# A fused decode attention kernel: the first load of B's output weights as transfers of 64, 51 and 13 rows

## The chip, the cores and the metric

The kernel runs on one core of one Trainium2 chip. The metric is the device time of one execution in microseconds (us), taken as the median of several runs. A second source is the profile: one execution recorded by the hardware profiler, with a start time and a duration for the instructions of every engine and for the packets of the DMA queues. In the profile PE is TensorE (PEld its weight loads), DVE is VectorE, ACT is ScalarE, POOL is GpSimd and SP is SyncE, which in this kernel does little but issue DMA transfers. A "q" behind an engine's name is its sequencer, so SPq is SP issuing a transfer or waiting on a semaphore. The core has 16 DMA engines; the page gives their mean busy share.

## What is computed

Two attention layers of one decode step, one after the other, their outputs set side by side. Both have a batch of 4, one query position, a model width of 512, 32 query heads of width 128 and a cache of 8192 positions. Layer A has 8 key/value heads, each shared by 4 query heads, and looks only at the last 2048 positions (`W`). Layer B has 32 key/value heads and looks at all 8192.

```python
def _B_ref(x, k_cache, v_cache, wq, wo):
    q = (x @ wq).reshape(B, Sq, H, Dh) ...            # 4 x 1 x 512 times 512 x 4096
    scores = jnp.einsum("bhqd,bhkd->bhqk", q, k_cache) * (Dh ** -0.5)
    p = _softmax(scores, axis=-1)
    o = jnp.einsum("bhqk,bhkd->bhqd", p, v_cache)
    return o ... .reshape(B, Sq, H * Dh) @ wo         # 4096 x 512 output weights
# _A_ref is the same with k and v cut to the last W positions and repeated over 4 query heads
return jnp.concatenate([a, b], axis=-1)
```

All tensors are bf16. B's keys and values alone are 537 MB, read once.

## The kernel before

**Chunks.** The work is cut into 40 chunks. Chunks 0 to 7 (`c < NCA`) are A's eight key/value heads, all four batch rows at once. Chunks 8 to 39 are B's: four heads (`hq` counts the groups of four heads) of one batch row, so that four chunks in a row share one `hq`. A chunk's keys are loaded to `kv` in SBUF, transposed on PE against an identity matrix (`emit_T`, line 555, matmuls of line 501), copied from PSUM to `kt` by DVE or ACT (lines 578 and 576), and multiplied with the query (`emit_S`, line 595, matmuls of line 503). Then come the softmax statistics, the exponentials, and the product with the values (`emit_pv`, line 747).

**Output weights.** B's `wo` is used in pieces of 512 rows, one for each `hq`. `dma_wos` (line 367) loads such a piece to the tile `wos`: 128 partitions, four weight rows of 512 in each, so one partition's row is 4096 bytes and one load is 512 KB. `reorder` (line 834) of each B chunk multiplies `wos` with a selection matrix `back` on PE, and `take_wol` copies the result to `wol`; `emit_fin` multiplies the chunk's attention output with `wol` at the chunk's end. A's own output weights go to the tile `wor` by `dma_wo` (line 359), also 512 KB a load.

**Order of loads.** SP issues nearly every transfer, in an order that is written out in lines 468 to 489: A's keys, values and output weights first, then for each B chunk the keys (`dma_kB`) and the values (`dma_vB`), with `dma_wos` ahead of the keys of every fourth B chunk. At the very end stand the output weights of A's last two heads (`LATEWO`). A transfer that reuses a buffer waits on SP for the engine that frees it, and everything behind it on SP waits too. `dma_wos(0)`, which has nothing to wait for, stands behind the values of A's chunk 7 and ahead of the keys of chunk 8, which are loaded as three pieces.

**Completion.** Each transfer raises a semaphore by 16 when it has landed. `add_dma` (line 93) counts the uses of a semaphore, and a key names the count at which a load is complete. POOL waits for these counts and passes them on to PE through counters (`land_wos`, `land_kB`, `land_vB`, issued by `relay` at line 82), one load after the other in the order of chunks. PE waits for `("wr", c)`, the counter that `land_wos` raises, ahead of the first reorder matmul of a chunk.

Of the kernel before, what the change touches and what calls it, by code (L numbers as in the profile page):

```python
# [13 lines left out]
P = 128  # L14
# [3 lines left out]
NH = 10  # L18
NWO = 2
LATEWO = 2  # L20
NPB = 2
NSM = 2
SLAG = 2
# [155 lines left out]
def bass_concat_heads__sliding_block_cached__mha_block_cached__decode_kernel(  # L179
# [30 lines left out]
    NCA = Hkv  # L210
# [13 lines left out]
    sch = _Sched()  # L224
    with ExitStack() as es:
        block = es.enter_context(nc.Block())

        def sb(name, shape, dt):
            return es.enter_context(nc.sbuf_tensor(name, shape, dt))

        def ps(name, shape, dt):
# [4 lines left out]
        wos = sb("wos", [P, 4, DO], BF16)  # L236
# [29 lines left out]
        pm = sb("pm", [P, HB, NB, 4], F32)  # L266
        pbt = {0: sb("pba", [P, NPB, NTA * 16 + NW], BF16), 1: sb("pbb", [P, 2, NTB * 2 + NW], BF16)}
        oT = sb("oT", [P, NSM, 16], BF16)
# [35 lines left out]
            waits=["c_onesf", "c_identf"], key="c_ind")  # L304
# [45 lines left out]
        def dma_wq(ab, at):  # L350

            waits = take(("wq", ab), at, 2, ("qmm", ab))
            src = WQ[ab].rearrange("(p r) n -> p (r n)", r=KC)
            sch.add_dma("sp", lambda e: e.dma_start(flat(at, 2), src), "d_h%d" % at, waits=waits, key=("wq", ab))
# [4 lines left out]
        def dma_wo(g):  # L359

            src = A_wo[g * 4 * P:(g + 1) * 4 * P, :].rearrange("(p r) n -> p (r n)", r=4)
            slot = wo_slot(g)
            dst = wor[:, slot, :]
            sch.add_dma("sp", lambda e: e.dma_start(dst, src), "d_wo%d" % slot,
                        waits=[("fin", g - 2)] if g >= 2 else [], key=("wo", g))

        def dma_wos(hq):


            src = B_wo[4 * hq * P:4 * (hq + 1) * P, :].rearrange("(p r) n -> p (r n)", r=4)  # L370
            sch.add_dma("sp", lambda e: e.dma_start(wos[:, :, :].rearrange("p r n -> p (r n)"), src), "d_wos",
                        waits=[("reord", NCA + 4 * hq - 1, 3)] if hq else [], key=("wos", hq))

        def dma_A(kind, c):
            ch = chunks[c]
# [62 lines left out]
        def dma_vB(c):  # L438

            ch = chunks[c]  # L440
            src = B_v[ch["b"], 4 * ch["hq"]:4 * ch["hq"] + 4].rearrange("u (pp j) d -> (u pp) (j d)", pp=P // 4)
            dst = flat(VB, 4)
            pieces = vpieces(c)
            fam = "d_v%d_" % len(pieces)
            j0 = 0
            for i, n in enumerate(pieces):
                waits = held[4] + held[5] + held[6] + held[7] if c == NCA else [("pv", c - 1, 0 if j0 + n <= NTB // 2 else 1)]
                x = slice(j0 * P, (j0 + n) * P)
                sch.add_dma("sp", lambda e, x=x: e.dma_start(dst[:, x], src[:, x]), fam + str(i), waits=waits, key=("v", c, i))
                j0 += n  # L450
# [21 lines left out]
        for c in range(NCA):  # L472
# [3 lines left out]
            if c == 2:  # L476
                dma_wq(1, 6)
            if c != 1 and c < NCA - LATEWO:
                dma_wo(c)
# [3 lines left out]
        for c in range(NCA, NC):  # L483
            if (c - NCA) % NB == 0:
                dma_wos((c - NCA) // NB)
            dma_kB(c)
            dma_vB(c)
        for c in range(NCA - LATEWO, NCA):
            dma_wo(c)
# [9 lines left out]
        def pe_mm(o, l, r, start=True, stop=True, transpose=False, waits=(), key=None):  # L499
            if transpose:  # L500
                sch.add("pe", lambda e: e.transpose(o, l, r), waits, key)  # L501
            else:
                sch.add("pe", lambda e: e.matmul(o, l, r, start=start, stop=stop), waits, key)  # L503
# [223 lines left out]
        def spread_A(c, bs):  # L727

            for b in bs:
                sch.add("act", lambda e, b=b: e.activation(  # L730
                    probs_of(c).rearrange("p j (b c) -> p j b c", b=NB)[:, :, b, :], eA[:, c % 2, :].rearrange("p (j c) -> p j c", c=REP),
                    ACTF.Copy, scale=mk[:, b:b + 1]),
                    waits=[("exp1", c), "mk", ("c_pb", 0)] + ([("pv", c - NPB)] if c >= NPB else []) if b == 0 else [],
                    key=("exp", c) if b == NB - 1 else None)
# [117 lines left out]
        def emit_fin(c):  # L852
            ab = 0 if c < NCA else 1
            if ab == 1:
                ov = oz[:, :].rearrange("p (b u) -> p b u", b=NB)
                ops = [(ov[:, :, u], wol[:, u, :]) for u in range(4)]
                waits = ["c_oz", ("oT", c)]
            else:
                w = wor[:, wo_slot(c), :].rearrange("p (r n) -> p r n", r=4)
                ops = [(zA[:, c % 2, r * NB:(r + 1) * NB], w[:, r, :]) for r in range(4)]  # L860
                waits = [("z", c), ("wo", c)]

            for i, (l, r) in enumerate(ops):
                for h, (p0, x) in enumerate(out_halves(ab)):
                    pe_mm(fin[p0:p0 + NB, 0:DO // 2], l, r[:, x], start=False,
                          stop=i == len(ops) - 1 and c == NCA - 1, waits=waits if i == h == 0 else [],
                          key=("fin", c) if i == len(ops) - 1 and h == 1 else None)
# [172 lines left out]
        for p0, x in out_halves(1):  # L1040
            pe_mm(fin[p0:p0 + NB, 0:DO // 2], zz[:, :], sel4[:, 0:2, :].rearrange("p r x -> p (r x)"), start=False, key=("end", p0))
        for c in range(NCA - LATEWO, NCA - 1):
            emit_fin(c)
# [62 lines left out]
```

## Time and profile before

| what | value |
|---|---|
| median of 3 runs | 1369.17 us |
| lowest and highest run | 1368.85 and 1373.74 us |
| time of the profiled execution | 1368.99 us |
| span of the profiled execution (first to last instruction) | 1367.3 us |
| mean granted TensorE clock | 0.976 |
| PE busy, ACT busy, DVE busy (share of the span) | 89%, 41%, 54% |
| bytes read from HBM | 587.21 MB |

The profiled execution's own time is 1.69 us over its span, for what lies around the instructions, and 0.18 us under the median. The kernel moves 587 MB through the DMA engines, so the first things to read are the DMA engines' busy share and rate over the span, and then where PE waits for a load to land. Shares of a short window can come out above 1.00, since a packet is counted in the window in which it starts.

### The profile page before, as it was taken

The page shows a single profiled execution, that of the slowest core. Times are in us where ns is not written, and L with a number is a line of the kernel's source. Part 1 is how long each engine was busy: PE and PEld are TensorE (multiplying, and loading weights), DVE is VectorE, ACT ScalarE, POOL GpSimd, SP SyncE. Part 2 cuts the span into 40 slices and gives each one's busy share as a digit, 9 for nine tenths or more (in the row PEclk, how much of TensorE's full clock was granted, in tenths as well). Part 3 has the DMA queues.
Part 4 walks back from the last instruction along what each step waited for, and adds up shares of the span by engine and source line. Part 5 has one row for each costly group of instructions (what it writes and reads, how often), then busy time and mean ns, then how long its engine had stood idle before and what let it go on. Part 6 is the DMA issues. An engine that isn't in the chain of part 4 may idle for free.

```text
span 1367.3 us, 62934 instructions
## 1 busy us (share of the span) xinstructions
PE 1222.9 (89%) x27807; PEld 1126.6 (82%) x27843; DVE 731.9 (54%) x1495; ACT 555.0 (41%) x777; POOL 202.8 (15%) x84
## 2 busy tenths in 40 slices
PE   6688799989898999888989899889899898899998
PEld 5687698878887988888889888878898888888888
DVE  2575455545455555554555555545555555455565
ACT  2453344434344443333444344334444343344443
POOL 2000022222210222222101222221012222200000
PEclk9998999999999999999999999999999999999999
DMA  9999999999999999999999999999999999999998
GB/s 398 428 427 431 432 438 431 428 435 424 441 431 429 431 429 437 435 432 429 437 430 437 429 429 431 439 433 429 429 439 435 429 430 437 439 428 429 429 427 372
DMA packets 16629, 587.52 MB, mean 430 GB/s; under 512 B 1864, under 2 KB 1888, under 8 KB 3936
## 3 DMA queue, kind: packets, MB, share of 16 engines
q1 hardware_dynamic: 16576, 587.21, 99.7%
q8 instruction: 15, 0.25, 0.1%
q14 instruction: 6, 0.05, 0.0%
q10 hardware_dynamic: 32, 0.01, 0.0%
HBM read 587.21 MB, written 0.01 MB: 429 GB/s over the span
## 4 chain that ended last, share of the span: by engine, by line
DMA 57%; PE 38%; issue 2%; DVE 2%; ACT 1%; SPq 0%; ACTq 0%; POOLq 0%; DVEq 0%
DMA kv<-in_B_k_cache_dram 51%; PE tr L501 22%; PE sc L503 10%; DMA kv<-in_A_k_cache_dram 4%; PE tr L503 3%; DMA kv<-in_B_v_cache_dram 2%; PE po L503 2%; PE ms L503 1%; PE fin L503 0%; DVE kt L578 0%; DVE sA L631 0%; ACT pbb L700 0%; PE sc L933 0%; ACT pba L730 0%; PE ms L501 0%
## 5 line engine op out<-in xcount | busy, mean ns | idle before, releaser
L501 PE MATMUL tr<-identb,kv 128*128 128x128 bf16 x8704 | 672.1, 223 | 48.5 <-POOLq L82 35.7
L578 DVE COPY kt<-tr 128x1024 bf16<-128x1024 bf16 x736 | 502.8, 691 | 320.3 <-PE tr L501 317.1
L501 PEld LDWEIGHTS tr<-identb,kv 128*128 128x128 bf16 x8704 | 520.9, 100 | 60.3 <-issue 52.0
L576 ACT ACTIVATE kt<-tr 128x1024 bf16<-128x1024 bf16 x352 | 359.3, 1023 | 455.4 <-PE tr L501 453.2
L503 PE MATMUL sc<-qq,kt 128*128 128x64 bf16 x8192 | 401.1, 192 | 11.1 <-DVE kt L578 9.4
L503 PEld LDWEIGHTS sc<-qq,kt 128*128 128x128 bf16 x8192 | 330.7, 98 | 17.7 <-DVE kt L578 12.7
L425 POOL COPY kv<-kv 128x4096 int32<-128x4096 int32 x54 | 193.0, 3602 | 988.4 <-DMA kv<-in_B_k_cache_dram 988.4
L700 ACT ACTIVATE pbb<-sc,negb 32x128 bf16<-32x128 f32 x256 | 137.9, 539 | 134.3 <-DVE negb L682 131.5
L503 PE MATMUL tr<-pbb,kv 128*128 128x64 bf16 x4096 | 135.8, 193 | 28.1 <-ACT pbb L700 25.5
L503 PEld LDWEIGHTS tr<-pbb,kv 128*128 128x128 bf16 x4096 | 131.1, 99 | 31.9 <-issue 29.7
L503 PE MATMUL po<-pbb,kv 128*128 128x64 bf16 x4096 | 135.0, 194 | 4.3 <-issue 4.3
L503 PEld LDWEIGHTS po<-pbb,kv 128*128 128x128 bf16 x4096 | 127.5, 98 | 5.4 <-issue 4.4
L848 ACT ACTIVATE wol<-tr 128x512 bf16<-128x512 f32 x32 | 19.1, 597 | 203.4 <-PE po L503 203.4
L850 DVE CAST wol<-tr 128x512 bf16<-128x512 f32 x64 | 41.2, 686 | 54.8 <-PE tr L503 54.8
L933 PE MATMUL sc<-sel,identb 128*128 128x512 bf16 x167 | 51.1, 384 | 13.6 <-issue 13.6
L933 PEld LDWEIGHTS sc<-sel,identb 128*128 128x128 bf16 x167 | 16.2, 97 | 48.6 <-issue 38.5
L707 DVE TENSOR_REDUCE rs<-pbb 128x4 f32<-128x512 bf16 x32 | 22.0, 687 | 50.1 <-ACT pbb L700 50.1
L780 DVE RECIPROCAL ib<-ms 128x8 f32<-128x8 f32 x32 | 6.6, 208 | 58.1 <-PE ms L503 58.1
L503 PE MATMUL tr<-wos,back 32*128 32x512 bf16 x384 | 34.8, 383 | 0.6 <-issue 0.5
L503 PE MATMUL po<-wos,back 32*128 32x512 bf16 x128 | 33.9, 384 | 0.0
L668 DVE TENSOR_REDUCE gm<-ms 4x4 f32<-4x128 f32 x72 | 19.8, 275 | 23.3 <-PE ms L501 23.3
L648 DVE TENSOR_REDUCE rh<-sc 128x4 f32<-128x512 f32 x32 | 22.1, 692 | 14.3 <-PE sc L503 14.3
(92 smaller groups left out, 506.2 us busy)
## 6 DMA issues: line engine op xcount, KB each, us to landing
kv<-in_B_v_cache_dram SPq DMA_DIRECT2D x10, 4096.0 KB, 24.1
kv<-in_B_k_cache_dram SPq DMA_DIRECT2D x7, 4096.0 KB, 19.7
kv<-in_A_k_cache_dram SPq DMA_DIRECT2D x8, 2048.0 KB, 15.8
kv<-in_A_v_cache_dram SPq DMA_DIRECT2D x8, 2048.0 KB, 16.7
kv<-in_B_k_cache_dram SPq DMA_DIRECT2D x6, 2048.0 KB, 26.2
kv<-in_B_v_cache_dram SPq DMA_DIRECT2D x3, 2048.0 KB, 29.9
kv<-in_A_wq_dram SPq DMA_DIRECT2D x1, 4096.0 KB, 12.5
wor<-in_A_wo_dram SPq DMA_DIRECT2D x8, 512.0 KB, 21.2
```

The costliest lines, as they stand in the source:

```text
L425: sch.add("pool", lambda e, dst=dst, org=org: e.tensor_copy(dst, org), waits=[("T", s0 + ch["NG"] - 1)] if g == QC[0] else [])
L501: sch.add("pe", lambda e: e.transpose(o, l, r), waits, key)
L503: sch.add("pe", lambda e: e.matmul(o, l, r, start=start, stop=stop), waits, key)
L576: sch.add("act", lambda e: e.activation(dst, src, ACTF.Copy), waits=waits, key=("ev", s))
L578: sch.add("dve", lambda e: e.tensor_copy(dst, src), waits=waits, key=("ev", s))
L648: sch.add("dve", lambda e: e.tensor_reduce(out=dst, in_=src, axis=AX.X, op=ALU.max), waits=[("S", ch["s"] + (half + 1) * ch["NG"] // 2 - 1 ...
L668: sch.add("dve", lambda e: e.tensor_reduce(out=gm[0:C, m, 0:U], in_=src, axis=AX.X, op=ALU.max), waits=[key_of("trm", c, half)], key=key_o ...
L700: sch.add("act", lambda e, src=src, dst=dst, pp=pp, u=u: e.activation(dst, src, ACTF.Exp, bias=negb[pp, half, u:u + 1], scale=scale), wait ...
L707: sch.add("dve", lambda e: e.tensor_reduce(out=dst, in_=probs_of(c, half).rearrange("p j u -> p u j"), axis=AX.X, op=ALU.add), waits=[("ex ...
L848: sch.add("act", lambda e, u=u, o=o: e.activation(wol[:, u, :], o, ACTF.Copy), waits=[("reord", c, u)], key=("wol", c, u))
L850: sch.add("dve", lambda e, u=u, o=o: e.tensor_copy(wol[:, u, :], o), waits=[("reord", c, u)], key=("wol", c, u))
L933: return e.matmul(sc[:, 1, :], identb[:, :], sel4[:, :, :].rearrange("p r x -> p (r x)"), start=True, stop=True)
```

## The change

The first load of `wos` (`hq` of 0) is issued as three transfers in place of one: partitions 0 to 63, 64 to 114 and 115 to 127. All three raise the semaphore `d_wos`, and the key that `land_wos` waits for stands on the third, so the count waited for is 48 where it was 16. The seven later loads of `wos` stay one transfer each; the counts that they are waited for at are 32 higher. The bytes, their places in SBUF, the queue (SP) and the place in the order of loads stay the same.

```diff
+UNEVEN = (64, 51, 13)
...
             src = B_wo[4 * hq * P:4 * (hq + 1) * P, :].rearrange("(p r) n -> p (r n)", r=4)
-            sch.add_dma("sp", lambda e: e.dma_start(wos[:, :, :].rearrange("p r n -> p (r n)"), src), "d_wos",
-                        waits=[("reord", NCA + 4 * hq - 1, 3)] if hq else [], key=("wos", hq))
+            dst = wos[:, :, :].rearrange("p r n -> p (r n)")
+            waits = [("reord", NCA + 4 * hq - 1, 3)] if hq else []
+            if hq == 0:
+                rows = 0
+                for n in UNEVEN:
+                    x = slice(rows, rows + n)
+                    rows += n
+                    sch.add_dma("sp", lambda e, x=x: e.dma_start(dst[x, :], src[x, :]), "d_wos", key=("wos", hq) if rows == P else None)
+                return
+            sch.add_dma("sp", lambda e: e.dma_start(dst, src), "d_wos", waits=waits, key=("wos", hq))
```

## The prediction

> **What bounds the kernel now.** I read the page's span and DMA lines first, then the busy shares by stretch, then the chain of waits, and last SP's timeline around the changed load.
>
> ```profile
> span 1367.3 us, 62934 instructions
> ...
> DMA packets 16629, 587.52 MB, mean 430 GB/s; under 512 B 1864, under 2 KB 1888, under 8 KB 3936
> ...
> q1 hardware_dynamic: 16576, 587.21, 99.7%
> ...
> q10 hardware_dynamic: 32, 0.01, 0.0%
> ```
>
> The packets of SP's queue (q1) fill 99.7% of what 16 DMA engines have in this span. There is almost no idle DMA time from which a loss could be paid.
>
> ```profile
> core 0: us, PE busy (x) PEld busy (x) DVE busy (x) ACT busy (x) POOL busy (x), PEclk, DMA share, GB/s
> ...
> 180.00:240.00 60.00, 55.09 (x1274) 51.79 (x1272) 33.49 (x65) 26.65 (x39) 7.14 (x2) 0.97 1.01 437
> 240.00:250.00 10.00, 8.75 (x178) 6.36 (x176) 2.99 (x11) 1.08 (x2) 0.99 (x1) 1.00 0.95 400
> ...
> 400.00:800.00 400.00, 363.52 (x8187) 332.56 (x8198) 211.88 (x416) 160.35 (x223) 75.37 (x22) 0.98 1.00 434
> 800.00:1200.00 400.00, 365.67 (x8333) 337.13 (x8341) 215.25 (x421) 163.35 (x225) 74.72 (x21) 0.98 1.00 433
> 1200.00:1330.00 130.00, 123.05 (x2939) 114.51 (x2941) 74.70 (x152) 57.15 (x82) 0.00 (x0) 1.00 1.00 429
> ```
>
> The last two columns are the DMA share and the rate. The engines are full in every long stretch; PE has 8 to 9% to spare. The one stretch with a hole is 240 to 250, with a share of 0.95: 0.5 us of ten, a mean over the engines.
>
> ```profile
> 181.86 28.16 DMA kv<-in_B_k_cache_dram
> 210.19 2.74 PE tr L501 x24
> 222.16 26.63 DMA kv<-in_B_k_cache_dram
> 249.04 1.51 PE tr L501 x24
> ```
>
> ```profile
> 1327.74 34.05 DMA kv<-in_B_v_cache_dram
> ...
> 1361.89 1.34 PE tr L503 x34
> ```
>
> These are pieces of the chain of waits: start, duration, what. A B chunk's keys issued at 181.86 land at 210.02 and PE's transposes follow at 210.19; the next land at 248.79 and PE follows at 249.04. The last values land at 1361.79 and PE follows 0.1 us later. So from B's early chunks to the end, DMA sets the pace, and since each of these loads is spread over many engines, it is the last engine's share that PE waits for. A DMA engine that falls behind by some time in mid-kernel holds everything up by that time, unless it meets a hole.
>
> **The change part by part.** First the price of a row.
>
> ```profile
> wor<-in_A_wo_dram SPq DMA_DIRECT2D x8, 512.0 KB, 21.2
> ...
> wos<-in_B_wo_dram SPq DMA_DIRECT2D x8, 512.0 KB, 23.9
> ...
> out_dram<-outsb ACTq DMA_DIRECT2D x2, 2.0 KB
> xs<-in_A_x_dram ACTq DMA_DIRECT2D x1, 4.0 KB
> xs<-in_B_x_dram ACTq DMA_DIRECT2D x1, 4.0 KB
> ```
>
> Sixteen loads of 512 KB have 16 x 128 rows, and the packets from 2 KB to under 8 KB are 3936 - 1888 = 2048: a row of 4096 bytes is one packet. At the mean rate one engine moves 430 / 16 = 26.9 GB/s, so a row takes 4096 / 26,900 = 0.152 us. A second way comes from the loads of `wor` at the end:
>
> ```profile
> L364 SPq DMA_DIRECT2D wor<-in_A_wo_dram x8: 333/383/593, 3.3 to 1328.7; - x8
> ...
> DMA to landing us min/median/max: 9.1/21.2/35.5
> ```
>
> The last one is issued at 1328.7 and, taking the longest landing of 35.5 for it, lands at 1364.2. Two such loads (SP's last ones) stand behind the values that landed at 1361.79, so 2 x 8 rows on each engine took 2.4 us: 0.15 us a row again.
>
> Now the split. One load of 128 rows gives 16 engines 8 rows each. How 51 and 13 rows are dealt out no row shows. What the profile has is ACT's queue, q10: four transfers of four rows (two of `xs`, two of the output) made 32 packets, 8 each, which fits 4 data rows and 4 completion records, so four engines with one row each. Equal shares are all I see. Dealt equally, 64 rows go to 16 engines (4 each), 13 rows to 13 engines (1 each), and 51 = 3 x 17 rows to three engines, 17 each. Bounds from both sides: at best 51 rows lie on 13 or more engines with at most 4 each, and the fullest engine has 4 + 4 + 1 = 9 rows, one more than now, +0.15 us. At worst 51 and 13 rows each lie on one engine, the same one: 4 + 51 + 13 = 68, 60 more than now, +9.1 us. I take equal shares as the form nearest to the rows: three engines with 4 + 17 + 1 = 22 rows, 14 more than now, 14 x 0.152 = +2.1 us on them; the other engines have 4 or 5 rows, so 3 or 4 fewer, -0.46 to -0.61 us.
>
> [...] No run here yet shows a row count that 16 does not divide and that is over 4.
>
> Does a lag of 2.1 us reach the end? Nothing in the kernel gives a lagging engine less work later. Two things take from it: the hole at 240 to 250 (0.5 us), where an engine that is late would not have idled, and the lag that the engines have against each other already, of which no view tells me which engine has it. Were the three engines the first to finish before, by up to 2.6 us, the change would only fill their lead. I take off the 0.5 us of the hole and nothing for the lead: +1.6 us, between -0.6 (the lead hides all, and the lightened engines set the end) and +2.1.
>
> SP and the relays:
>
> ```profile
> 99.69 0.59 SPq L371 DMA_DIRECT2D wos<-in_B_wo_dram  x1
> 100.33 6.30 SPq L410 DMA_DIRECT2D kv<-in_B_k_cache_dram  x3
> 120.38 0.80 SPq L449 DMA_DIRECT2D kv<-in_B_v_cache_dram  x2
> ```
>
> ```profile
> L371 SPq DMA_DIRECT2D wos<-in_B_wo_dram x8: 327/328/594, 99.7 to 1181.4; - x8
> ...
> DMA to landing us min/median/max: 11.7/23.9/24.7
> ```
>
> ```profile
> 121.46 0.63 PE L503 MATMUL tr<-wos,back 32*128 32x512 bf16 x3 [0.50 <-issue]
> ```
>
> Two more issues at 0.33 to 0.59 us delay what is queued behind them on SP, B's first keys and then values, by 0.7 to 1.2 us: 100.33 becomes at most 101.5. These keys' bytes have their turn only behind `wos`, which lands at 99.69 + 11.7 = 111.4 (the shortest landing is this load's), so 10 us of queued transfers hide the issues; without that cover the price is up to 1.2 us. POOL's relay for `wos` comes at most 2.1 + 1.2 us later, 114.7; PE's first reorder matmul is at 121.46, so 6.8 us remain, and without them the chunk would start up to 3.3 us late. Behind that relay on POOL stand the relays of the first keys, which land later than `wos` anyway. The later counts on `d_wos` are waited for as before. No instruction of PE, DVE or ACT is added.
>
> [...]
>
> The sum, against the profiled execution: 1368.99 + 2.1 - 0.5 + 0 + 0 = **1370.6 us**. The median of the runs is 0.18 us above that execution, which lies well inside the range.
>
> **The rivals.** (1) The lag is hidden: the three engines had a lead, or the rows are dealt evenly. For it speaks the hole, which shows that not all engines are late all the time; against it that the hole is 0.5 us, and that with a share of 1.00 no engine can have had much rest. Time: 1368.99 - 0.6 to + 0.3, about 1369.0. (2) Slower beyond what can be told from no change: the 51 rows lie on one engine. With 13 rows elsewhere it has 4 + 51 + 1 = 56 rows, 48 more: +7.3 us, 1376.3; with 13 there too, 1378.1. It decides from 45 more rows on one engine (6.85 / 0.152). For it: 51 is odd, and no row here shows a split in three. Against: the four-row transfers were dealt out over four engines. [...] (4) Faster: engines out of step disturb each other less, and the rate rises. From 112 us on some 1251 us are left; at 437 in place of 433 GB/s they would be 11.5 us shorter, with the lag about 1359.6. Against: rate and share rise together (437 at 1.01, 434 at 1.00, 400 at 0.95), so a busy engine has one rate, near 433 GB/s over 16, and there is nothing to win.
>
> **How the numbers follow.** Forecast 60%, lag hidden 23%, a fixed price 5%, one engine 8%, a better rate 4%. About 0.5% (6.8 us) is what a measurement of this kernel tells from no change; the first three cases lie within it: same 0.88, slower 0.08, faster 0.04. The range takes in the hidden lag and the fixed price, 1368.2 to 1373.2, and leaves out the 12% of the last two. The likeliest case's own range is 1369.5 to 1371.3.
>
> **What would show it.** The packets from 2 KB to under 8 KB stay 2048, SP's queue still fills over 99% of the span, and SP shows three transfers of `wos` near 99.7 with the keys' issue about 1 us later. The small packets under 512 B would rise by 3 + 13 = 16 by equal shares, since each engine that takes part writes one completion record, and by only 2 if the 51 and 13 rows lie on one engine each. The chain of waits should have the last values land 1 to 2 us later than 1361.79, with PE following within 0.1 us as now. Wrong would be: a hole in the DMA share after 112 us wider than that at 240 to 250, a first reorder matmul later than 122 us, or a DMA rate in the stretches 400 to 1200 that differs from 433 and 434 GB/s by more than 2.

## The result, and the profile after

| | before | after |
|---|---|---|
| median of 22 runs | 1368.94 us | 1372.06 us |
| lowest and highest run | 1368.4 and 1373.74 us | 1371.45 and 1373.74 us |
| span of the profiled execution | 1367.3 us | 1371.0 us |

The ratio is 1.0022, with a 95% interval from 1.0017 to 1.0028: the change costs 3.1 us. It is clear of the runs' scatter, and under the 0.5% that the prediction took as the least change worth the name. The forecast was 1370.6 us.

First the page after, span and DMA lines.

```profile
span 1371.0 us, 62936 instructions
...
DMA packets 16645, 587.52 MB, mean 429 GB/s; under 512 B 1880, under 2 KB 1904, under 8 KB 3952
...
q1 hardware_dynamic: 16592, 587.21, 99.7%
```

Still 2048 packets from 2 KB to under 8 KB (3952 - 1904), the same bytes, the same 99.7% of busy DMA time. The small packets (under 512 B) rose by 1880 - 1864 = 16, the 3 + 13 of equal shares: by this count the 51 rows lie on three engines.

Next SP's timeline around the changed load, with start, duration and what.

```profile
99.37 1.52 SPq L379 DMA_DIRECT2D wos<-in_B_wo_dram  x3
100.93 5.38 SPq L419 DMA_DIRECT2D kv<-in_B_k_cache_dram  x3
120.05 0.80 SPq L458 DMA_DIRECT2D kv<-in_B_v_cache_dram  x2
```

Three issues in 1.5 us; B's keys are issued at 100.93 where it was 100.33, its values at 120.05 where it was 120.38. SP's cost is hidden, as expected.

Then the chain of waits after, at the places that were shown of before.

```profile
184.01 28.16 DMA kv<-in_B_k_cache_dram
...
224.33 26.62 DMA kv<-in_B_k_cache_dram
```

```profile
1331.50 34.01 DMA kv<-in_B_v_cache_dram
...
1365.60 1.34 PE tr L512 x34
```

The keys that were issued at 181.86 are issued at 184.01 and take the same 28.16 us; they land 2.2 us later. The next ones land at 250.95, 2.2 us after the 248.79 of before; the last values land at 1365.51, 3.7 us after 1361.79. PE still follows within 0.1 us. The rates of the long stretches did not move:

```profile
240.00:250.00 10.00, 8.48 (x199) 6.53 (x196) 3.28 (x12) 3.12 (x8) 0.00 (x0) 1.00 0.98 413
400.00:800.00 400.00, 362.34 (x8146) 331.61 (x8152) 210.14 (x413) 159.45 (x222) 72.25 (x21) 0.97 1.00 433
800.00:1200.00 400.00, 364.60 (x8300) 335.92 (x8310) 214.82 (x420) 162.49 (x224) 77.89 (x22) 0.98 1.00 433
```

So 2.2 us went before 240 us. The rest shows only later and unevenly: keys issued at 338.12 before are issued 2.3 us later after (340.38), those at 727.81 are 3.1 us later (730.93), the last values 3.7 us; part of that is the profiled execution of after itself, which at 1372.75 us lies 0.7 us above its median. Busy times in short windows around the changed load find where the delay starts; the last two columns are the DMA share and the rate in GB/s. Before:

```profile
107.00:108.00 1.00, 0.72 (x22) 0.47 (x17) 0.62 (x2) 0.47 (x2) 0.00 (x0) 1.00 0.95 401
108.00:112.00 4.00, 2.88 (x95) 2.59 (x91) 2.97 (x8) 0.00 (x0) 0.00 (x0) 1.00 1.04 436
112.00:114.00 2.00, 1.45 (x42) 1.35 (x42) 1.40 (x7) 0.00 (x0) 0.00 (x0) 1.00 1.00 426
114.00:115.00 1.00, 1.00 (x45) 1.00 (x42) 0.52 (x2) 0.80 (x2) 0.00 (x0) 0.80 0.96 410
```

and after:

```profile
107.00:108.00 1.00, 0.79 (x27) 0.80 (x28) 0.30 (x2) 0.15 (x1) 0.00 (x0) 1.00 1.13 389
108.00:112.00 4.00, 2.85 (x96) 2.57 (x93) 3.25 (x9) 0.00 (x0) 0.00 (x0) 1.00 1.00 237
112.00:114.00 2.00, 1.48 (x49) 1.38 (x46) 1.27 (x6) 0.15 (x1) 0.00 (x0) 1.00 1.02 246
114.00:115.00 1.00, 1.00 (x45) 1.00 (x42) 0.60 (x2) 0.97 (x3) 0.00 (x0) 0.67 0.87 303
```

From 108 to 114 us the DMA engines are as busy as ever, a share of 1.00, and move 237 to 246 GB/s in place of 426 to 436. All 16 engines together are slow while the rows of the cut load are in flight; a share of 1.00 at half the rate means that packets take longer, not that engines wait for work. The trace also keeps the duration of each packet, and shows this directly: of the packets of 16 KB, which belong to the loads beside `wos`, every one that starts from 108 to 114 us takes 0.90 to 1.33 us, where it took 0.61 to 0.63 before; a row of `wos` takes 0.20 to 0.47 us where it took 0.16 to 0.17. Against the 426 GB/s that stood at a share of 1.00 before, the loss over the four windows is (37 + 4 x 189 + 2 x 180 + 123) / 426 = 3.0 us. That is nearly all of the 3.1 us. Where it comes from, whether from the uneven share, from the number of transfers, or from where the rows go, the trace alone does not tell.

### The profile page after: what moved, and what is told of

It reads as the page before. It is cut to its first block, busy times and chain, and to the rows that moved or that the text cites. A ratio compares the mean times of both kernels' runs of the same rounds, so it can differ in the third digit from the quotient of the medians.

```text
span 1371.0 us, 62936 instructions
## 1 busy us (share of the span) xinstructions
PE 1222.4 (89%) x27807; PEld 1126.2 (82%) x27843; DVE 732.0 (53%) x1495; ACT 555.5 (41%) x777; POOL 203.0 (15%) x84
## 2 busy tenths in 40 slices
DMA packets 16645, 587.52 MB, mean 429 GB/s; under 512 B 1880, under 2 KB 1904, under 8 KB 3952
## 3 DMA queue, kind: packets, MB, share of 16 engines
q1 hardware_dynamic: 16592, 587.21, 99.7%
## 4 chain that ended last, share of the span: by engine, by line
DMA 58%; PE 38%; issue 2%; DVE 2%; ACT 1%; SPq 0%; ACTq 0%; POOLq 0%; DVEq 0%
DMA kv<-in_B_k_cache_dram 52%; PE tr L510 22%; PE sc L512 10%; DMA kv<-in_A_k_cache_dram 4%; PE tr L512 3%; DMA kv<-in_B_v_cache_dram 2%; PE po L512 1%; PE ms L512 1%; PE fin L512 0%; DVE sA L640 0%; PE sc L942 0%; DVE kt L587 0%; ACT pbb L709 0%; ACT pba L739 0%; PE ms L510 0%
## 5 line engine op out<-in xcount | busy, mean ns | idle before, releaser
L585 ACT ACTIVATE kt<-tr 128x1024 bf16<-128x1024 bf16 x352 | 359.6, 1024 | 457.5 <-PE tr L510 455.4
```

Source lines behind the costliest of these rows:

```text
L585: sch.add("act", lambda e: e.activation(dst, src, ACTF.Copy), waits=waits, key=("ev", s))
```

## The experiments

Two theories at first. *Uneven share*, the prediction's: the fullest engines have 14 rows too many and hold the rest up. *Slow stretch*: as long as rows of a load that is cut across the partitions are in flight, all engines are slow, evenly shared or not. Every time below is a median, beside the median of the kernel before on the same chip; every ratio is that of the two, with its 95% interval.

### Two even halves (e1)

```diff
-UNEVEN = (64, 51, 13)
+UNEVEN = (64, 64)
```

> The first load of wos as two transfers of 64 partitions. Both divide evenly over 16 engines, 4 rows each, so every engine has 8 rows as before and no engine is left behind. Theory 'uneven share' (the loss is what the fullest engine has too much): no change, within 0.3 us of the kernel before, DMA rate in 108 to 112 us near 430 GB/s. Theory 'slow stretch' (while rows of a load that is cut across the partitions are in flight, all 16 engines together run at little over half their rate, 237 in place of 436 GB/s in the changed kernel): a stretch at 220 to 300 GB/s of 2.3 to 4.6 us (8 rows of 0.29 us, and the lag of the engines against each other), and 1.1 to 2.0 us slower than before.

Measured: 1371.27 us beside 1369.32, ratio 1.0016 (1.0007 to 1.0025), +2.0 us. The windows of this kernel:

```profile
108.00:112.00 4.00, 2.85 (x96) 2.57 (x93) 3.19 (x9) 0.00 (x0) 0.00 (x0) 1.00 1.01 239
112.00:114.00 2.00, 1.48 (x39) 1.37 (x36) 1.20 (x7) 0.00 (x0) 0.00 (x0) 0.56 0.98 315
114.00:115.00 1.00, 1.00 (x44) 1.00 (x41) 0.52 (x2) 0.81 (x2) 0.00 (x0) 0.50 1.04 442
```

By equal shares no engine has a row too many, and the rate falls to 239 all the same; it is back by 114 us, about one microsecond sooner than in the change, whose fullest engines have 22 rows, by the prediction's estimate, and not 8. The uneven share is not what makes the loss; at most it makes the stretch longer.

### Three transfers by columns (e2)

```diff
-UNEVEN = (64, 51, 13)
+UNEVEN = (1024, 816, 208)
...
-                    sch.add_dma("sp", lambda e, x=x: e.dma_start(dst[x, :], src[x, :]), "d_wos", key=("wos", hq) if rows == P else None)
+                    sch.add_dma("sp", lambda e, x=x: e.dma_start(dst[:, x], src[:, x]), "d_wos", key=("wos", hq) if rows == 4 * DO else None)
```

> Three transfers for the first load of wos as in the change, but each has all 128 partitions and a part of the columns (1024, 816 and 208 of 2048). If the number of transfers costs (issue, completion, a fixed price each): as much as the change, +3.1 us. Theory 'uneven share': 0 to +0.3 us. Theory 'slow stretch', in which only a cut across the partitions matters: 0 to +0.3 us too, and a rate in 108 to 112 us over 400 GB/s (rows of 416 bytes move a little worse).

Measured: 1369.48 us beside 1369.32, ratio 1.0001 (0.9992 to 1.001).

```profile
108.00:112.00 4.00, 2.85 (x96) 2.57 (x93) 3.25 (x9) 0.00 (x0) 0.00 (x0) 1.00 1.05 416
```

The rate of 416 stands beside 436 before; as to short rows, in the trace before packets of 1024 bytes (the loads of `xs`) take 0.044 to 0.046 us, some 23 GB/s for one engine, where those of 4096 take 0.159 us, 26 GB/s. Three transfers on one semaphore, each with all 128 partitions, cost nothing that can be measured here. This ends the number of transfers, their issue on SP and a fixed price for each as causes.

### The same row counts in another order (e3)

```diff
-UNEVEN = (64, 51, 13)
+UNEVEN = (51, 13, 64)
```

> The same three row counts in the order 51, 13, 64, so that the 51 rows lie on partitions 0 to 50 in place of 64 to 114 and each engine has as many rows as in the change. Theory 'uneven share': +3.1 us as the change. Theory 'slow stretch': +3.1 us too if any cut across the partitions does it, with 220 to 260 GB/s in 108 to 112 us; under 2 us, and a rate over 300 GB/s for most of the stretch, if what counts is that the first engines write to the upper half of the partitions.

Measured: 1371.74 us beside 1369.32, ratio 1.0018 (1.0009 to 1.0027), +2.4 us.

```profile
108.00:112.00 4.00, 2.85 (x95) 2.58 (x92) 3.09 (x9) 0.00 (x0) 0.00 (x0) 1.00 1.06 245
112.00:114.00 2.00, 1.48 (x47) 1.38 (x47) 1.41 (x7) 0.00 (x0) 0.00 (x0) 1.00 0.92 233
```

The slow stretch is there as well, with the 51 rows on partitions 0 to 50. The interval overlaps that of the change, so nothing is made of the 0.7 us between them.

### The lag alone (e4)

The load is one transfer again. Three engines are to get 59 KB each more than the others through three-row transfers into a spare tile. The page has 126 packets more on q1 than before (16702 and 16576), two for each of the 63 rows: a data row and a completion record, which fits three engines for each transfer. That these are the same three every time, and that their rows go to partitions which the same engine has in a load of 128 rows, are assumptions of the author in this run and in those built on it: no trace here names the engine of a packet. Left out of the edit below are the name of a semaphore for these transfers and a wait for it at the kernel's end.

```diff
+        spare = sb("spare", [P, 11 * P], BF16)
...
-            if hq == 0:
-                rows = 0
-                for n in UNEVEN:
...
+            if hq < 3:
+                for i in (0, 1, 2, 3, 32, 33, 34):
+                    sch.add_dma("sp", lambda e, i=i: e.dma_start(spare[i:i + 9:4, :], A_k[0, 0, 0:33, :].rearrange("(p r) n -> p (r n)", r=11)), "d_spare",
+                                waits=[("spare", hq - 1)] if hq and i == 0 else [], key=("spare", hq) if i == 34 else None)
             sch.add_dma("sp", lambda e: e.dma_start(dst, src), "d_wos", waits=waits, key=("wos", hq))
```

> The first load of wos is one transfer of 128 rows again. Ahead of each of the first three loads of wos stand seven transfers of three partitions (i, i+4, i+8) of 2816 bytes each into a spare tile that nothing reads: 21 x 2816 bytes more for three engines, 59 KB, as much as the 14 rows (57 KB) that the change gives the fullest engines, and 59,136 / 26,900 = 2.2 us. Theory 'uneven share': +1.5 to +2.2 us, with the DMA rate elsewhere as before. Theory 'slow stretch': a lag alone costs the same at most, and the rest of the change's +3.1 us is not here; no stretch of 107 to 115 us under 380 GB/s.

Measured: 1369.16 us beside 1369.32, ratio 1.0 (0.9991 to 1.0009).

```profile
108.00:112.00 4.00, 2.85 (x95) 2.57 (x90) 2.99 (x9) 0.00 (x0) 0.00 (x0) 1.00 1.03 431
```

2.2 us more work on three engines (the same three, by the assumption above), in three portions of some 0.7 us, cost nothing that can be measured, and there is no slow stretch. The way of the lag to the end, which the prediction reckoned with, fails here if the assumption holds; a lag of 2.1 us at one place, without a cut load, was not tried.

### The same transfers on other partitions (e5)

```diff
-                for i in (0, 1, 2, 3, 32, 33, 34):
+                for i in (64, 65, 66, 67, 96, 97, 98):
...
```

> The kernel of e4 with one difference: the 21 transfers of three rows of 2816 bytes go to the partitions i, i+4, i+8 from 64, 65, 66, 67, 96, 97 and 98 on, where e4 had 0, 1, 2, 3, 32, 33 and 34; rows, bytes, source and places in the order are the same. In e4 there was no slow stretch (431 GB/s in 108 to 112 us) and no loss. Theory 'wrong partitions' (the slow stretch comes when an engine writes to partitions that are another engine's in a load of 128 rows): a stretch at 220 to 300 GB/s of about 1.4 us for each of the three groups of seven (7 x 2816 bytes at 14 GB/s), in the first one within 105 to 109 us, and +1 to +3 us in all. Rival 'any load on few engines, or cut in its rows, by its source or its descriptors': as e4, no slow stretch and within 0.3 us of the kernel before.

Measured: 1372.13 us beside 1369.06, ratio 1.0021 (1.0012 to 1.003), +3.1 us. First this kernel, then that of the lag alone, in the windows of the first group of seven:

```profile
108.00:109.00 1.00, 1.00 (x41) 1.00 (x38) 0.73 (x2) 0.00 (x0) 0.00 (x0) 1.00 0.99 225
109.00:110.00 1.00, 1.00 (x43) 1.00 (x40) 0.93 (x3) 0.00 (x0) 0.00 (x0) 1.00 0.92 305
```

```profile
108.00:109.00 1.00, 1.00 (x42) 1.00 (x38) 0.38 (x1) 0.00 (x0) 0.00 (x0) 1.00 1.00 411
109.00:110.00 1.00, 1.00 (x42) 1.00 (x39) 0.93 (x3) 0.00 (x0) 0.00 (x0) 1.00 1.03 425
```

Rows, bytes, source and number of transfers are the same in both; the destination partitions alone differ, and with them 225 GB/s stand against 411. The 177 KB of these transfers cost what the whole change costs. So in these transfers it is the place in SBUF that makes the slow stretch. That the same makes it in the cut load is inferred, from the same fall of the rate and the same length of the packets; the loads of `wos` cut across the partitions that are read here (the change's, e1's, e3's and the second of e7) all have the stretch.

### More lag on the same three engines (e6)

```diff
-            if hq < 3:
+            if hq < 8:
```

> The transfers of e4 ahead of all eight loads of wos, not of the first three alone: 56 rows of 2816 bytes more on three engines, 158 KB or 5.9 us of their time, spread over the kernel. Theory 'the three engines had a lead' (e4 cost nothing because these engines were up to some 2.3 us ahead, and idled in holes): +1 to +3.6 us, with the DMA rate at 430 GB/s around each group. Rival 'a lag of some engines never reaches the end, since the others give them time': within 0.4 us of the kernel before.

Measured: 1373.41 us beside 1369.06, ratio 1.0031 (1.0019 to 1.0042), +4.4 us (2.6 to 5.7 by the interval), against 5.9 us of added work. The rival, within 0.4 us, falls; the theory of a lead had +1 to +3.6. That theory's condition, a rate of 430 GB/s around each group, did not hold everywhere:

```profile
864.00:884.00 20.00, 17.94 (x395) 15.39 (x392) 9.40 (x20) 6.69 (x11) 7.15 (x2) 1.00 1.01 423
800.00:1200.00 400.00, 365.20 (x8286) 336.78 (x8294) 214.01 (x419) 162.48 (x224) 75.82 (x22) 0.98 1.00 431
```

Before, 800 to 1200 had 433 GB/s; 2 GB/s less are 400 x 2 / 433 = 1.8 us. In two places, near 872 and 1187 us, packets of 64 KB take up to 3.76 and 3.97 us, where the usual is 2.42; over the whole run 108 of them take more than 2.49 us, and 48 before. So a part of the 4.4 us is slower packets and not the lag itself, for a reason that stays open. That more of these transfers cost something is shown; how much lag three engines can hide is not (5.9 - 4.4 = 1.5 us by the medians, 0.2 to 3.3 by the interval), nor whether the 2.1 us of the change are hidden in full.

### All eight loads cut (e7)

```diff
-            if hq == 0:
-                rows = 0
-                for n in UNEVEN:
...
+            rows = 0
+            for n in UNEVEN:
+                x = slice(rows, rows + n)
+                rows += n
+                sch.add_dma("sp", lambda e, x=x: e.dma_start(dst[x, :], src[x, :]), "d_wos", waits=waits, key=("wos", hq) if rows == P else None)
```

> All eight loads of wos are cut in 64, 51 and 13 rows. Theory 'slow stretch': each cut load costs as much as the first, 8 x 3.1 = +25 us, with 210 to 260 GB/s for some 7 us in each group of chunks; somewhat less, +15 us, where the neighbouring loads of 64 KB rows keep the engines closer together. Theory 'uneven share' as the prediction had it: 8 x 2.1 = +17 us less the holes, at a rate near 430 GB/s for the other engines. If the first place alone is special (A's last values and B's first pieces beside it): +3 to +5 us.

Measured: 1420.87 us beside 1369.06, ratio 1.0382 (1.0366 to 1.0398), +51.8 us, twice what the slow stretch was expected to give. The busy windows around the second cut load of this kernel:

```profile
264.00:268.00 4.00, 4.00 (x88) 3.92 (x86) 3.23 (x7) 1.47 (x3) 0.00 (x0) 1.00 1.32 462
268.00:272.00 4.00, 4.00 (x99) 4.00 (x96) 2.74 (x4) 3.88 (x7) 0.00 (x0) 1.00 1.14 289
272.00:276.00 4.00, 3.71 (x112) 3.54 (x110) 2.51 (x5) 0.88 (x1) 0.00 (x0) 1.00 0.76 206
276.00:280.00 4.00, 3.17 (x98) 2.99 (x93) 1.63 (x6) 2.47 (x6) 0.00 (x0) 1.00 0.93 371
```

and in its chain of waits, and on its page

```profile
261.72 35.93 DMA kv<-in_B_k_cache_dram
```

```profile
q1 hardware_dynamic: 16704, 587.21, 98.7%
```

The slow stretch lasts some 12 us here, not 7. (A packet of 64 KB takes some 2.42 us before, up to 4.56 us here, and is counted where it starts, so the share in one window of 4 us says little: 1.32 in one and 0.76 in another.) Before, the keys behind the second load of `wos` landed 29.29 us after their issue (259.49); here it is 35.93. If the first cut costs 3.1 us as in the change, the seven others cost (51.8 - 3.1) / 7 = 7.0 us each. Not all of it is slow packets: SP's queue leaves 1.3% of 1417.3 us of the engines' time unfilled here and 0.3% of 1367.3 us before, which is 14 us more, or 2 us of the 7.0. The neighbours of these loads are rows of 64 KB in place of the 16 KB ones beside the first load; whether it is that which raises the price was not tried alone.

### Neighbouring partitions (e8), and a shift by four (e9)

Both are the kernel of the lag alone with other destinations, all below partition 64. If any other destination than that of the lag alone made a slow stretch, both would have one; if only the half from 64 on did, neither would.

```diff
-                for i in (0, 1, 2, 3, 32, 33, 34):
-                    sch.add_dma("sp", lambda e, i=i: e.dma_start(spare[i:i + 9:4, :], A_k[0, 0, 0:33, :].rearrange("(p r) n -> p (r n)", r=11)), "d_spare",
+                for i in (0, 4, 8, 12, 32, 36, 40):
+                    sch.add_dma("sp", lambda e, i=i: e.dma_start(spare[i:i + 3, :], A_k[0, 0, 0:33, :].rearrange("(p r) n -> p (r n)", r=11)), "d_spare",
```

> The kernel of e4 again, with the three rows of each of the 21 transfers on neighbouring partitions i, i+1, i+2 (i of 0, 4, 8, 12, 32, 36, 40) in place of i, i+4, i+8. Nothing goes to the partitions from 64 on, where e5's slow stretch came from. [...] Rival 'only the other half': as e4, within 0.3 us of the kernel before.

Measured: 1369.79 us beside 1369.22, ratio 1.0004 (0.9995 to 1.0013).

```diff
-                    sch.add_dma("sp", lambda e, i=i: e.dma_start(spare[i:i + 9:4, :], A_k[0, 0, 0:33, :].rearrange("(p r) n -> p (r n)", r=11)), "d_spare",
+                    sch.add_dma("sp", lambda e, i=i: e.dma_start(spare[i + 4:i + 13:4, :], A_k[0, 0, 0:33, :].rearrange("(p r) n -> p (r n)", r=11)), "d_spare",
```

> The kernel of e4 with each of the three-row transfers four partitions further: i+4, i+8, i+12 for the i of e4. [...] Rival 'only the other half': as e4, no slow stretch and within 0.3 us. [...]

Measured: 1371.6 us beside 1369.22, ratio 1.0017 (1.0008 to 1.0026), +2.4 us. (Its profiled execution took 1374.42 us, 2.8 above the median; the windows below are read for the rate alone.) The windows of the neighbouring partitions first, then those of the shift:

```profile
108.00:109.00 1.00, 1.00 (x41) 1.00 (x38) 0.59 (x2) 0.00 (x0) 0.00 (x0) 1.00 1.09 412
109.00:110.00 1.00, 1.00 (x43) 1.00 (x40) 0.93 (x3) 0.00 (x0) 0.00 (x0) 1.00 0.96 366
```

```profile
108.00:109.00 1.00, 1.00 (x41) 1.00 (x38) 0.48 (x1) 0.00 (x0) 0.00 (x0) 1.00 1.04 253
109.00:110.00 1.00, 1.00 (x42) 1.00 (x39) 0.93 (x2) 0.00 (x0) 0.00 (x0) 1.00 0.85 294
```

A shift by four partitions within the lower half is enough for 253 GB/s: "only the other half" falls. Three rows on neighbouring partitions disturb far less, 412 and 366 GB/s in these windows, and the time cannot be told from before: the first case, that any other destination is slow, misses there. Why the one shift is slow and the neighbouring partitions hardly are, no run shows.

## Why the prediction was right, and where it was wrong

The measured time lies in the range, and it is within 0.5% as the likeliest case had it. It is above the likeliest case's own range, 1369.5 to 1371.3; only a fixed price for each added transfer, of which more below, had carried the range that far up. The path to the number was wrong in its main term, so that it lies in the range is luck.

- **What bounds the kernel** was right: a loss in the DMA engines at 110 us is still there at the last landing, 3.7 us later than before in the profiled executions, with PE following within 0.1 us.
- **The split** was right: 16 more completion records, three engines for 51 rows by equal shares. That the three engines of the 51 rows are among the thirteen of the 13, which makes 22 rows, stays an estimate: no trace names the engine of a packet.
- **The term of +2.1 us, for 22 rows on three engines, reaching the end** is the step that failed. By the lag alone, 2.2 us more on three engines (the same three, by assumption) in three portions cost 0 with an interval of about 1.2 us to each side, and in the change the slow stretch by itself accounts for 3.0 of the 3.1 us (the 22 rows may make it longer, since two even halves cost 2.0). Rival (1), the lag is hidden, had this part right under that assumption; whether by a lead, as it supposed, is not shown. The prediction had no row for the lead and put it at nothing in the sum.
- **The price of a row, 0.152 us**, was taken from loads of 128 rows and held for the cut load without a bound. There it failed: from 108 to 114 us a row takes 0.30 us in the median, not 0.16, and the 16 KB packets beside it 1.07 us, not 0.61. The loss from that, 3.0 us by the windows, was in no term and no rival.
- **"A busy engine has one rate, near 433 GB/s over 16"**, the argument against rival (4), is where this could have been seen to be open. The rows behind it were all of loads with 128 partitions; the change is the first in this kernel with fewer of them in bulk. The rate did change, and downwards.
- **Two small sizes** were read a little off, and decide nothing: the packet of a row takes 0.159 us in the trace before, not 0.152; and the hole of 0.5 us at 240 to 250 us is a share of packets by their starts, where with each packet's time counted where it lies the engines idle for 0.16 us on average.
- **SP, the relays, PE's first use**: right. The keys are issued 0.6 us later, the values no later, and the first reorder matmul starts at 121.1 us.
- **A fixed price for each added transfer**, which has 5% of the chances and its place in the range, is shown by no run: three transfers by columns cost 0.2 us more than the kernel before, between -1.1 and +1.4 by the interval.
- **One engine with all 51 rows**, rival (2), falls by the count of records.

Among the signs that it named, the prediction had the rate of the long stretches, which stayed, and not the rate at the change itself; the last values, which it had landing 1 to 2 us later, land 3.7 us later. The forecast of 1370.6 was 1.5 us off: two errors, +1.6 us for a lag that costs about nothing and 0 for a slow stretch that costs 3.0, went against each other.

## What to carry to other kernels

In this kernel the DMA engines ran at about 430 GB/s with loads into SBUF that have all 128 partitions; a cut of one load across the partitions slowed the transfers in flight beside it (237 GB/s for all together, 0.90 to 1.33 us for a packet of 16 KB in place of 0.61 to 0.63), at 3 us for one 512 KB load and some 7 us for each of seven more beside bigger rows, while a cut by columns cost nothing that can be measured (0.2 us). A busy share of 1.00 did not tell how fast the DMA engines move bytes (237 and 426 GB/s were both seen at it): read the share and the rate together, in windows as short as the change itself. Prices taken from a trace hold for the forms that are in it, and a change of form needs a bound of its own.

## What was not expected

That so few bytes disturb so many: in the transfers on far partitions 21 x 3 rows of 2816 bytes, 177 KB of 587 MB, cost 3.1 us, and engines that by equal shares have no row of them were slow too, if the three that have are always the same: 13 engines at their full rate alone would have moved 13 x 26.9 = 350 GB/s, and all 16 moved 225 at a share of 0.99. All seven packets of 16 KB that start in that window take 0.87 to 1.26 us; with the lag alone the fourteen in it take 0.61 to 0.63. Which destinations do this is seen case by case, in the same two windows: with the lag alone 411 and 425 GB/s, on neighbouring partitions 412 and 366, four partitions further 253 and 294, from partition 64 on 225 and 305. Why some are slow and others not, and why packets of other transfers are slowed as well, no run here shows; both stay open.
